# Block-sparse attention and a GELU layer on one core: loading weights with casting DMAs from GpSimd

## The chip, the core and the metric

The kernel runs on one core of a Trainium2 chip. A core has a matrix engine (TensorE, PE in the profile), three engines for elementwise work (VectorE or DVE, ScalarE or ACT, GpSimd or POOL) and SyncE (SP), which here only issues DMAs. Each engine works through its own queue in program order; 16 DMA engines move the data between main memory (HBM) and the on-chip memory SBUF. TensorE writes to PSUM, from where VectorE or ScalarE bring results to SBUF. The metric is the device time of one execution in microseconds (us), the median of several runs.

## The reference

Inputs are q, k and v of shape (4, 8, 768, 64) and the two weights, `w_in` (512, 2048) and `w_out` (2048, 512), all float32.

```python
def _attn_ref(q, k, v):                      # block = 64, 12 blocks, top_k = 3
    k_rep = k.reshape(B, H, n_blocks, block, D).mean(axis=3)
    gate_scores = np.einsum('bhsd,bhnd->bhsn', q, k_rep)
    gate_scores = np.where(causal, gate_scores, -1000000000.0)
    top_idx = np.argsort(gate_scores, axis=-1)[..., -top_k:]
    ...
            sel = set(top_idx[b, h, i].tolist()) | {own_block[i]}
            for kb in sel:
                mask[b, h, i, kb * block:(kb + 1) * block] = True
    ...
    mask = mask & (pos[:, None] >= pos[None, :])
    scores = np.where(mask, scale * np.matmul(q, k.transpose(0, 1, 3, 2)), -1000000000.0)
    attn = softmax(scores)
    return np.matmul(attn, v)

def _moe_ref(x, w_in, w_out):
    h = x @ w_in
    g = 0.5 * h * (1.0 + np.tanh(c * (h + 0.044715 * h * h * h)))
    return g @ w_out
```

Every query attends, causally, to its own block of 64 keys and to the three blocks whose mean key it scores highest. The heads are put side by side to x of 3072 x 512, which goes through `w_in`, a GELU and `w_out`.

## The kernel before

The 32 heads are taken as 16 pairs, p = 4b + hp for batch b. Pairs 0 to 3 (batch 0) are each worked through in three units of 256 queries; pairs 4 to 15 in one unit of 768. A unit loads q, k, v as float32, splits q and k into a high and a low fp16 part, computes the gate scores, picks the blocks, builds the mask, computes the scores, takes exponentials, multiplies with v and writes normalised rows, transposed, to `xT` (fp16). The GELU layer runs over 12 chunks of 256 tokens: for four quarters of the hidden size an up-projection (`hps` in PSUM), a GELU to `gT`, and for two halves of 128 tokens a down-projection over the four quarters into `ops`. A chunk of the GELU layer needs its batch's four pairs, so in the run the attention of one batch and the GELU layer of earlier tokens are interleaved.

The program is a table of named steps and one long string, `ORDER`, that says in which order they are emitted. Since every engine keeps program order, the string is the schedule of each engine and of each DMA queue. A suffix `:a`, `:v` or `:p` picks the engine (ACT, DVE, POOL), `@0` to `@2` a PSUM buffer. The steps that the rest of this text names:

- `d0.g.t.x` loads q, k or v (x = 0, 1, 2) of 128 tokens of four heads of batch 0, `d.p.x` those of a pair of a later batch (two DMAs, one for each head), both into float32 tiles of the pool `io`. They are issued on SP, but for four early k loads on ACT.
- `lw.in.s` and `lw.out.s`, s = 0 to 7, load an eighth of `w_in` or `w_out`, 128 x 1024 float32, into a staging tile of the pool `w32` (7 buffers), issued on SP (line 329). `cw.in.s` and `cw.out.s` cast it to fp16 (line 338), on POOL all 16. Quarter dj of the up-projection needs eighths 2dj and 2dj + 1 of `w_in`, quarter dj of the down-projection those of `w_out`.
- `v.p.t` casts v to fp16 in one of four `v16` tiles, whose 65th column holds ones (`c.v`). `hn0`/`hn1` and `ln0`/`ln1` are the high and low parts of q and k for pairs 4 to 15, `zqh`, `zkh` and `zql` transposes by DMA, `c0`/`c1` copies of the transposes.
- `t2` transposes q and k of batch 0 on PE; `k` computes scores on PE, `ma` adds the mask there, `x` takes exponentials on ACT, `a` zeroes what lies above the diagonal on POOL (two instructions each for the units of batch 0, one otherwise), `p` multiplies with v on PE.
- `u.ch.dj.half` is the up-projection on PE (8 matmuls for each half), `y` the GELU on ACT, `f.ch.ti.dj` four matmuls of the down-projection, `o` the copy of its result out of PSUM, `w` the store, issued on SP.
- `c.*` fill constants, most of them on POOL. `dmN` runs N matmuls of zeros that nothing reads. `c.warm` runs 40 of the same kind and is the last step but one of the order.

Of the kernel before, what the change touches and what calls it, by code (L numbers as in the profile page):

```python
# [8 lines left out]
FP32 = mybir.dt.float32  # L9
# [17 lines left out]
c.ident d0.0.0.0 d0.0.1.0 d0.0.0.1 c.ident16 c.v.0 c.bd c.par.1 c.par.0 d0.0.1.1 c.kb.3 c.own  # L27
c.kb.1 d0.1.1.0 t2.1.0@0 d0.0.2.0 c.kb.0 c.v.1 d0.1.0.0 c.kb.2 t2.0.0@1 s.1.0 d0.1.1.1 c.erow.0
d0.1.0.1 b.1.0 h2.1.0 l.1.0 h2.0.0 d0.0.2.1 c.gate s.0.0 c.v.2 dm13 g.1.0 m.1.0 t2.2.0@2 c.erow.3
d0.0.3.0 t2.3.0@0 mt.1.0 l.0.0 c.erow.1 mc.1.0:a s.2.0 d0.1.2.0 d0.1.0.2 d0.0.3.2 b.0.0 dm10 g.0.0  # L30
d0.0.3.1 s.3.0 c.erow.2 k.1.0.0@1 h2.2.0 d0.0.1.2 m.0.0 d0.0.0.2 h2.3.0 c.v.3 d0.0.5.0 v.1.0:p
d0.1.3.0 dm16 mt.0.0 l.3.0 ma.1.0.0 mc.0.0:a l.2.0 d0.1.1.2 t2.1.2@0 v.0.0:p b.3.0 dm6 g.3.0 c.bi
x.1.0.0 t2.0.2@2 dm7 k.0.0.0@1 h2.0.2 ma.0.0.0 b.2.0 m.3.0 x.0.0.0 g.2.0 d0.1.2.1 d0.1.3.1 s.0.2
lw.in.0 h2.1.2 m.2.0 dm14 k.2.0.0@1 mt.3.0 b.0.2 mc.3.0:a lw.in.1 a.1.0.0 dm8 mt.2.0 l.0.2
mc.2.0:a d0.0.5.1 dm8 ma.2.0.0 lw.in.4 cw.in.0:p g.0.2 t2.3.2@2 d0.0.2.2 l.1.2 a.0.0.0 s.1.2
d0.0.4.0 k.0.2.0@0 x.2.0.0 v.2.0:p h2.3.2 d0.1.5.0 k.3.0.0@1 lw.in.2 ma.3.0.0 m.0.2 s.3.2 x.3.0.0
a.3.0.0 dm8 mt.0.2 a.2.0.0 l.3.2 dm6 k.0.2.1@1 v.3.0:p mc.0.2:a b.1.2 p.0.0.0@2 p.0.0.1 ma.0.2.0
x.0.2.0 g.1.2 x.0.2.1 n.0.0 dm6 t2.2.2@2 lw.out.0 p.1.0.0@0 m.1.2 p.1.0.1 d0.0.4.1 n.1.0 h2.2.2
dm7 xt.0.0 lw.in.3 lw.in.6 lw.out.1 p.3.0.0@1 l.2.2 p.3.0.1 xc.0.0:a dm8 mt.1.2 s.2.2 b.3.2
v.1.2:p d0.1.4.0 k.1.2.0@0 v.0.2:p mc.1.2:a dm5 xt.1.0 k.1.2.1@2 xc.1.0:a cw.in.1:p ma.1.2.0 n.3.0  # L40
x.1.2.1 cw.in.2:p lw.in.5 dm2 g.3.2 x.1.2.0 dm3 p.2.0.0@1 p.2.0.1 a.0.2.1 dm4 t2.0.4@2 d0.1.4.1
lw.in.7 m.3.2 a.1.2.1 dm4 xt.3.0 n.2.0 cw.out.0:p p.0.2.0@0 h2.0.4 p.0.2.1 xc.3.0:a dm5 xt.2.0
lw.out.2 t2.1.4@1 n.0.2 d.4.1 xc.2.0:a d0.1.2.2 b.2.2 u.0.0.0@0 cw.in.4:p cw.in.3:p h2.1.4
cw.in.5:p s.0.4 l.0.4 g.2.2 m.2.2 u.0.0.1 y.0.0 u.0.1.0@2 mt.2.2 b.0.4 cw.out.1:p u.0.1.1 mc.2.2:a
g.0.4 cw.in.7:p d0.1.3.2 s.1.4 l.1.4 cw.in.6:p m.0.4 lw.out.3 k.2.2.0@0 k.2.2.1@1 ma.2.2.0 y.0.1
p.1.2.0@2 d0.1.5.1 mt.3.2 mc.3.2:v v.3.2:p x.2.2.0 p.1.2.1 f.0.0.0 xt.0.2 n.1.2 k.3.2.0@2 lw.out.5
k.3.2.1@0 cw.out.2:p ma.3.2.0 d.5.1 x.2.2.1 b.1.4 xc.0.2:v mt.0.4 lw.out.4 d0.1.4.2 u.0.2.0@1
a.2.2.1 lw.out.6 hn1.4.0:v mc.0.4:v d.4.0 x.3.2.1 u.0.2.1 x.3.2.0 g.1.4 ln1.4.0:v v.2.2:v y.0.2
u.0.3.0@0 u.0.3.1 k.0.4.2@2 p.2.2.0@1 p.2.2.1 m.1.4 cw.out.3:p ma.0.4.1 a.3.2.1 cw.out.5:p s.4.0
y.0.3 t2.2.4@0 d0.1.5.2 n.2.2 t2.3.4@1 b.4.0 x.0.4.2 xt.2.2 xc.2.2:v h2.3.4 xt.1.2 s.2.4 f.0.0.1  # L50
p.3.2.0@2 p.3.2.1 d0.0.4.2 hn1.5.0:p h2.2.4 s.3.4 d0.0.5.2 l.3.4 l.2.4 n.3.2 k.0.4.0@1 xc.1.2:a
mt.1.4 k.0.4.1@0 mc.1.4:a ma.0.4.0 k.1.4.2@2 ma.1.4.1 b.2.4 x.0.4.0 lw.out.7 xt.3.2 xc.3.2:v
cw.out.4:p a.0.4.2 ln1.5.0:v f.0.0.2 g.2.4 x.0.4.1 d.5.0 x.1.4.2 k.1.4.0@1 k.1.4.1@0 ma.1.4.0
x.1.4.1 x.1.4.0 hn0.4.0:p m.2.4 cw.out.6:p u.1.0.0@2 mt.2.4 b.3.4 mc.2.4:v ln0.4.0:v cw.out.7:p
u.1.0.1 s.5.0 b.5.0 u.1.1.0@0 y.1.0 v.0.4:p g.3.4 k.2.4.0@1 m.3.4 u.1.1.1 c.ke.0.0:p v.2.4:v
zqh.4.0 f.0.0.3 p.0.4.0@2 y.1.1 p.0.4.1 v.1.4:v k.2.4.1@0 o.0.0:a ma.2.4.0 zql.4.0 n.0.4
c.ke.0.1:p c.q0.0 mt.3.4 zkh.4.0 mc.3.4:v f.0.1.0 hn0.5.0:v xt.0.4 k.2.4.2@2 ma.2.4.1 a.1.4.2
xc.0.4:v f.0.1.1 x.2.4.1 g.4.0 x.2.4.2 ln0.5.0:v d.6.1 c.ke.1.1:p x.2.4.0 f.0.1.2 k.3.4.2@0
ma.3.4.1 hn1.6.0:p k.3.4.0@2 k.3.4.1@1 zql.5.0 v.3.4:v c.q0.1 ma.3.4.0 c1.4.0.0:p zqh.5.0 x.3.4.2
x.3.4.1 c0.4.0.0:p m.4.0 ln1.6.0:v d.6.0 a.2.4.2 f.0.1.3 x.3.4.0 c0.4.0.1:v d.7.1 u.1.2.0@0 mt.4.0  # L60
mc.4.0.0:a hn0.6.0:p c0.5.0.0:p zkh.5.0 u.1.3.0@1 p.1.4.0@2 mc.4.0.1:v p.1.4.1 o.0.1:a g.5.0
u.1.3.1 u.1.2.1 c1.4.0.1:v c0.5.0.1:p a.3.4.2 w.0.0 n.1.4 zqh.6.0 y.1.3 k.4.0.3@2 y.1.2 c1.5.0.0:p
f.1.0.0 p.2.4.0@1 p.2.4.1 m.5.0 c.ke.1.0:p n.2.4 x.4.0.3 ln0.6.0:v d.7.0 f.1.0.1 k.4.0.1@0 s.6.0
b.6.0 x.4.0.1 k.4.0.4@1 p.3.4.0@2 p.3.4.1 xt.1.4 k.4.0.0@0 f.1.0.2 zql.6.0 xc.1.4:v hn1.7.0:v
c1.5.0.1:p a.4.0.3 mt.5.0 n.3.4 x.4.0.4 k.4.0.2@1 x.4.0.0 mc.5.0.1:v k.4.0.5@2 f.1.0.3 x.4.0.5
mc.5.0.0:v k.5.0.0@0 d.4.2 c0.6.0.0:p x.4.0.2 xt.3.4 o.1.0:a x.5.0.0 a.4.0.0 k.5.0.2@2 k.5.0.4@1
ln1.7.0:v xc.3.4:v xt.2.4 x.5.0.4 zkh.6.0 f.1.1.0 c0.6.0.1:p xc.2.4:v g.6.0 a.4.0.1 a.4.0.4
u.2.1.0@0 u.2.1.1 v.4.0:p hn0.7.0:v a.4.0.5 u.2.0.0@1 u.2.0.1 a.4.0.2 d.8.1 x.5.0.2 p.4.0.0@2
y.2.1 m.6.0 k.5.0.5@0 ln0.7.0:v mt.6.0 mc.6.0.1:v y.2.0 p.4.0.1 mc.6.0.0:v f.1.1.1 k.5.0.1@1 s.7.0
hn1.8.0:p n.4.0 a.5.0.0 a.5.0.4 c1.6.0.0:p x.5.0.5 x.5.0.1 d.8.0 hn0.8.0:v k.5.0.3@0 u.2.2.0@2  # L70
u.2.3.0@1 ln1.8.0:v c1.6.0.1:p a.5.0.2 a.5.0.5 x.5.0.3 b.7.0 u.2.3.1 zqh.7.0 zql.7.0 ln0.8.0:v
g.7.0 m.7.0 a.5.0.1 u.2.2.1 y.2.3 f.1.1.2 d.5.2 k.6.0.5@0 a.5.0.3 k.6.0.0@1 y.2.2 k.6.0.4@2
c0.7.0.1:p f.1.1.3 w.0.1 zqh.8.0 x.6.0.5 s.8.0 zkh.7.0 v.5.0:p x.6.0.4 x.6.0.0 a.6.0.4 p.5.0.0@0
p.5.0.1 o.1.1:v k.6.0.1@2 b.8.0 x.6.0.1 c1.7.0.0:p mt.7.0 f.2.0.0 mc.7.0.0:a k.6.0.3@1 mc.7.0.1:v
c0.7.0.0:a f.2.0.1 k.6.0.2@2 zql.8.0 d.6.2 x.6.0.3 g.8.0 c1.7.0.1:v a.6.0.5 n.5.0 c0.8.0.1:p
x.6.0.2 a.6.0.3 a.6.0.0 d.9.1 v.6.0:p k.7.0.3@0 f.2.0.2 a.6.0.1 m.8.0 k.7.0.1@1 w.1.0 d.9.0
a.6.0.2 zkh.8.0 k.7.0.2@2 f.2.0.3 x.7.0.3 d.7.2 k.7.0.0@0 hn1.9.0:v xt.5.0 xc.5.0:v x.7.0.1
o.2.0:a p.6.0.0@1 p.6.0.1 ln1.9.0:v hn0.9.0:p x.7.0.0 a.7.0.3 x.7.0.2 d.10.0 xt.4.0 k.7.0.4@0
x.7.0.4 xc.4.0:v f.2.1.0 mt.8.0 c0.8.0.0:p c1.8.0.1:v mc.8.0.1:v zqh.9.0 a.7.0.1 k.7.0.5@2
ln0.9.0:v zql.9.0 w.1.1 n.6.0 f.2.1.1 mc.8.0.0:a a.7.0.4 v.7.0:a zkh.9.0 c1.8.0.0:p a.7.0.2 d.8.2  # L80
f.2.1.2 a.7.0.0 k.8.0.0@0 x.7.0.5 s.9.0 a.7.0.5 p.7.0.0@2 b.9.0 p.7.0.1 c0.9.0.1:p c0.9.0.0:p
c1.9.0.0:p d.10.1 x.8.0.0 xt.6.0 xc.6.0:a k.8.0.5@1 n.7.0 k.8.0.1@0 x.8.0.1 f.2.1.3 hn0.10.0:v
xt.7.0 a.8.0.0 xc.7.0:v k.8.0.2@2 x.8.0.5 a.8.0.5 k.8.0.4@0 u.3.0.0@1 x.8.0.2 v.8.0:p g.9.0
k.8.0.3@2 u.3.0.1 zqh.10.0 a.8.0.2 x.8.0.4 m.9.0 u.3.1.0@0 x.8.0.3 u.3.1.1 o.2.1:v a.8.0.3 d.11.1
a.8.0.4 u.3.2.0@2 mt.9.0 c1.9.0.1:p ln0.10.0:v a.8.0.1 mc.9.0.1:v y.3.0 hn1.10.0:p y.3.1
mc.9.0.0:a d.11.0 zql.10.0 u.3.2.1 f.3.0.0 k.9.0.1@1 p.8.0.0@0 ln1.10.0:v p.8.0.1 d.9.2 y.3.2
k.9.0.0@2 d.12.1 x.9.0.1 s.10.0 f.3.0.1 hn1.12.0:p k.9.0.2@1 f.3.0.2 n.8.0 zkh.10.0 b.10.0 x.9.0.0
k.9.0.5@0 k.9.0.4@2 x.9.0.2 c0.10.0.0:v x.9.0.5 u.3.3.0@1 x.9.0.4 k.9.0.3@0 hn0.11.0:v a.9.0.2
g.10.0 c0.10.0.1:v u.4.1.0@2 m.10.0 c1.10.0.1:p x.9.0.3 a.9.0.4 w.2.0 u.3.3.1 u.4.1.1 u.4.2.0@0
xt.8.0 a.9.0.1 a.9.0.0 a.9.0.3 d.12.0 v.9.0:p d.13.0 ln0.11.0:v u.4.2.1 xc.8.0:v y.3.3 y.4.2  # L90
f.3.0.3 hn1.11.0:v mt.10.0 u.4.0.0@1 u.4.0.1 o.3.0:v zqh.11.0 a.9.0.5 mc.10.0.0:v f.3.1.0
c1.10.0.0:v p.9.0.0@0 y.4.0 ln1.12.0:v f.3.1.1 hn0.12.0:v zkh.11.0 zql.11.0 y.4.1 mc.10.0.1:v
k.10.0.5@1 p.9.0.1 zqh.12.0 k.10.0.2@2 f.3.1.2 w.2.1 c0.11.0.0:p ln1.11.0:v x.10.0.5 x.10.0.2
n.9.0 s.11.0 b.11.0 k.10.0.1@1 zkh.12.0 d.10.2 u.5.2.0@0 s.12.0 k.10.0.0@2 x.10.0.1 c1.11.0.0:p
x.10.0.0 ln0.12.0:v k.10.0.4@1 d.13.1 b.12.0 g.11.0 f.3.1.3 a.10.0.2 k.10.0.3@2 a.10.0.5 x.10.0.4
d.11.2 a.10.0.1 x.10.0.3 u.5.2.1 hn0.13.0:a u.5.1.0@1 u.5.1.1 m.11.0 zql.12.0 mt.11.0 y.5.1
c1.11.0.1:v o.3.1:v hn1.13.0:p u.5.0.0@2 ln0.13.0:v u.5.0.1 c0.11.0.1:v u.4.3.0@1 u.4.3.1
mc.11.0.1:v f.4.0.0 mc.11.0.0:v zql.13.0 xt.9.0 y.5.2 c1.12.0.0:v w.3.0 d.14.0 c0.12.0.0:v
c1.12.0.1:p a.10.0.3 d.14.1 y.5.0 ln1.13.0:v xc.9.0:v k.11.0.3@0 y.4.3 f.4.0.1 g.12.0 k.11.0.1@2
# [38 lines left out]
def kernel(  # L138
# [9 lines left out]
    nc = tc.nc  # L148
# [8 lines left out]
    NPAIR = B * HP  # L157
# [744 lines left out]
```

## Time and profile before

| what | value |
|---|---|
| median of 3 runs | 285.09 us (284.98 to 286.42) |
| the profiled execution | 284.7 us, its span 282.7 us |
| TensorE clock granted | 1.00 over the whole span |
| PE matmuls | 2956, of them 140 of zeros by `dm`, 40 by `c.warm` |
| first up-projection `u.0.0.0` starts | 29.94 us |
| last w_out cast starts | 56.88 us |
| DMA read and written | 27.26 MB and 6.29 MB |
| weight loads to landing | 7.4 us (w_in), 7.0 us (w_out), median |

The span is the time between the first and the last thing that the profiler saw on the core; the execution's own time is 2.0 us longer. In the profile a line such as L338 is a line of the kernel. A busy share of an engine is an average over the span; rows of 40 digits give it for 40 equal slices, in tenths. A row of a group reads: line, engine, operation, output <- input, shapes, count, then busy time in us and mean ns of one, then the idle time of the engine just before these instructions and what ended it. The list of waits gives, for an engine and a tile, whom it waited for: us in total, times, the longest. SPq is the queue on which SP issues DMAs; the time of such a row is that of the issue, not of the transfer.

### The profile page before, as it was taken

Reading aid. Unit: us, or ns where it says so; the run is one execution under the profiler, and the core shown is the slowest. Engines: PE = TensorE matmul, PEld = TensorE weight load, DVE = VectorE, ACT = ScalarE, POOL = GpSimd, SP = SyncE. Lnnn points to the kernel's source line nnn. Section 1 sums busy time; section 2 is a strip of 40 time slices with the busy share of each in tenths; the row PEclk is TensorE's granted clock in tenths of the full one; section 3 lists DMA queues with packets and bytes.
Section 4 is the critical chain, followed back from the end, with each engine's and each line's share of the span. In section 5 each row is a group of like instructions: output and inputs, shape, how many; then the busy total and the mean of one; then the engine's idle time right before and its main releaser. Section 6 shows DMA issues by size and latency. Waiting matters only on the chain.

```text
span 282.7 us, 7360 instructions
## 1 busy us (share of the span) xinstructions
PE 267.8 (95%) x2956; PEld 191.2 (68%) x2956; DVE 159.7 (56%) x511; ACT 194.6 (69%) x222; POOL 139.2 (49%) x215
## 2 busy tenths in 40 slices
PE   3898998799999989989999999999999999999998
PEld 2776865557668756767778656688766666767655
DVE  3988788798888478746778697634503041000000
ACT  2466898679999987897488887877897721434130
POOL 8668476888999478473937671660110300000000
DMA  8999989888898893999999956991001102010111
GB/s 158 218 313 312 353 221 309 210 142 160 168 222 170 179 218 60 180 220 207 112 219 179 216 97 131 152 195 39 0 2 74 39 0 77 37 39 0 74 39 74
DMA packets 112097, 41.11 MB, mean 145 GB/s; under 512 B 104896, under 2 KB 104896, under 8 KB 112064
## 3 DMA queue, kind: packets, MB, share of 16 engines
q1 hardware_dynamic: 109952, 40.12, 68.3%
q10 hardware_dynamic: 2112, 0.52, 1.1%
q8 instruction: 23, 0.38, 0.6%
q14 instruction: 10, 0.08, 0.1%
HBM read 27.26 MB, written 6.29 MB: 119 GB/s over the span
## 4 chain that ended last, share of the span: by engine, by line
PE 75%; DMA 9%; POOL 5%; SPq 4%; DVE 3%; issue 2%; ACT 0%; ACTq 0%; POOLq 0%
PE ops L821 27%; PE hps L800 26%; PE st L623 8%; PE pv L705 6%; DMA io<-in_k_dram 4%; DMA io<-in_v_dram 3%; DMA io<-in_q_dram 2%; POOL at L691 2%; PE xt L734 2%; POOL hn L187 2%; SPq L356 1%; SPq L329 1%; PE mt L576 1%; PE kp L475 1%; DVE ln L435 1%
## 5 line engine op out<-in xcount | busy, mean ns | idle before, releaser
L821 PE MATMUL ops<-w_out,gT 128*128 128x512 f16 x384 | 94.6, 379 | 2.6 <-POOL w_out L338 2.0
L676 ACT ACTIVATE at<-st 128x1024 f16<-128x1024 f32 (+2 forms) x96 | 83.9, 917 | 13.9 <-PE st L623 8.5
L800 PE MATMUL hps<-xT,w_in 128*128 128x256 f16 x768 | 91.4, 272 | 0.0
L800 PEld LDWEIGHTS <-w_in 128*128 128x128 f16 x768 | 73.8, 98 | 13.4 <-issue 0.4
L810 ACT ACTIVATE gT<-hps 128x1024 f16<-128x1024 f32 x48 | 47.7, 1023 | 41.0 <-PE hps L800 40.6
L691 POOL TENSOR_SCALAR_AFFINE_SELECT at<-at 128x256 f16<-128x256 f16 x96 | 47.8, 520 | 36.8 <-ACT at L676 35.9
L821 PEld LDWEIGHTS <-gT 128*128 128x128 f16 x384 | 35.8, 97 | 35.9 <-issue 3.4
L623 PE MATMUL st<-qk,qk 76*128 76x512 f16 (+2 forms) x192 | 37.4, 305 | 1.2 <-DVE xn L721 1.0
L829 DVE COPY osb<-ops 128x512 f32<-128x512 f32 x16 | 11.0, 689 | 45.6 <-PE ops L821 43.5
L187 POOL TENSOR_SCALAR hn<-io 128x768 f16<-128x768 f32 x12 | 25.7, 2144 | 20.8 <-DMA io<-in_k_dram 11.1
L435 DVE SCALAR_TENSOR_TENSOR ln<-io,hn 128x768 f16<-128x768 f32 x24 | 27.6, 1152 | 4.7 <-POOL hn L187 4.4
L705 PEld LDWEIGHTS <-at 128*128 128x128 f16 x672 | 24.0, 98 | 4.0 <-POOL at L691 0.6
L705 PE MATMUL pv<-v,at 128*128 128x65 f16 x672 | 25.7, 194 | 0.5 <-POOL at L691 0.4
L623 PEld LDWEIGHTS <-qk 76*128 76x128 f16 x192 | 16.1, 97 | 10.6 <-issue 1.1
L676 ACT ACT_TABLE_LOAD x13 | 16.7, 1283 | 3.2 <-PE st L623 1.9
L810 ACT ACT_TABLE_LOAD x14 | 18.0, 1283 | 0.2
L721 DVE TENSOR_TENSOR xn<-pv,zrec 128x256 f16<-128x256 f32 (+1 forms) x24 | 16.6, 691 | 0.8
L458 POOL COPY qk<-khT 64x768 f16<-64x768 f16 x14 | 12.8, 915 | 7.4 <-DMA khT<-hn 3.8
L743 DVE COPY xT<-xt 128x768 f16<-128x768 f16 (+1 forms) x17 | 7.6, 446 | 14.6 <-PE xt L734 14.4
L586 DVE COPY qk<-mt 12x640 f16<-12x640 f16 x17 | 8.3, 486 | 11.9 <-ACT qk L586 9.9
L458 POOL COPY qk<-qhT 64x768 f16<-64x768 f16 x13 | 13.0, 999 | 3.6 <-issue 2.5
L554 DVE MAX8 mx<-gm 128x8 f32<-128x12 f32 x160 | 14.0, 158 | 0.8
(87 smaller groups left out, 293.1 us busy)
## 6 DMA issues: line engine op xcount, KB each, us to landing
out_dram<-osb SPq DMA_DIRECT2D x24, 256.0 KB, 2.6
io<-in_k_dram SPq DMA_DIRECT2D x24, 192.0 KB, 4.1
io<-in_q_dram SPq DMA_DIRECT2D x24, 192.0 KB, 4.1
io<-in_v_dram SPq DMA_DIRECT2D x24, 192.0 KB, 4.1
w_in<-in_moe_w_in_dram SPq DMA_DIRECT2D x8, 512.0 KB, 7.4
w_out<-in_moe_w_out_dram SPq DMA_DIRECT2D x8, 512.0 KB, 7.0
io<-in_q_dram SPq DMA_DIRECT2D x12, 128.0 KB, 4.3
io<-in_v_dram SPq DMA_DIRECT2D x12, 128.0 KB, 4.2
```

The lines of the kernel that those rows point to most:

```text
L187: math_on[eng].tensor_scalar(out=out, in0=in_, scalar1=c, scalar2=None, op0=ALU.mult)
L435: math_on[eng].scalar_tensor_tensor(out=g.rearrange("p t c -> p (t c)"), in0=IO[u[0], x].rearrange("p t h d -> p (t h d)"), scalar=QS, in1 ...
L458: copy_on[eng](out=dst[0:64, :], in_=src[64 * hh:64 * hh + 64, :])
L554: nc.vector.max(out=mx8[:, g, :], in_=gm[:, g, :])
L623: nc.tensor.matmul(st[:, hh, cb:cb + nq * 128], kt[p % 2][hh][0:64 + NBLK, jc * 128:(jc + 1) * 128], qt[p % 2][hh][0:64 + NBLK, qc * 128:( ...
L676: nc.scalar.activation(out=ov, in_=iv, func=AF.Exp, bias=0.0, scale=SCALE / (QS * QS))
L691: nc.gpsimd.affine_select(out=a, in_=a, compare_op=ALU.is_ge, fill=0.0, base=0, pattern=[[0, 2], [1, 128]], channel_multiplier=-1,)
L705: nc.tensor.matmul(pvt[:, o:o + 65], AT[p, hh, jc, qc], v16[p % NSLOT][:, jc, hh, :], start=(jc == 0), stop=(jc == qc),)
L721: nc.vector.tensor_tensor(out=xn[:, 0:nt].rearrange("p c h d -> p h c d"), in0=pz[:, :, :, 0:64], in1=zrec[:, :, 0:nt].unsqueeze(3).to_bro ...
L800: nc.tensor.matmul(hps[:, j * TCH:(j + 1) * TCH], w_in16[:, ci, fi * 128:(fi + 1) * 128], xT[ci][:, t0:t0 + TCH], start=(ci == 0), stop=(c ...
L810: nc.scalar.activation(out=g.rearrange("p a w -> p (a w)"), in_=G["h", ch, dj], func=AF.Gelu_apprx_tanh, bias=0.0, scale=1.0,)
L821: nc.tensor.matmul(G["o", ch, ti], G["g", ch, dj][:, j, ti * 128:(ti + 1) * 128], w_out16[:, fi, :], start=(fi == 0), stop=(fi == NF - 1),)
```

## The change

- The steps `cw.*` and the pool `w32` go. `lw.*` is now one DMA from the float32 weight straight into `w_in16` or `w_out16`, issued by GpSimd; the DMA casts.
- For pairs 14 and 15 `d.p.2` loads v in the same way, two DMAs, straight into `v16`; their steps `v.14.0` and `v.15.0` go.
- `io` and `atp` get 12 buffers instead of 9.
- `c.warm` goes.
- `ORDER` is a new one for all other steps as well, with other engines for some: high parts on POOL 16 instead of 12, v casts of 22 steps as 11 on POOL, 8 on ACT, 3 on DVE (before 15, 1, 8 of 24), output copies 15 on ACT and 9 on DVE (before 8 and 16). The `dm` steps hold 158 matmuls instead of 140.

```diff
-    io = ctx.enter_context(tc.tile_pool(name="io", bufs=9))
-    w32p = ctx.enter_context(tc.tile_pool(name="w32", bufs=7))
+    io = ctx.enter_context(tc.tile_pool(name="io", bufs=12))
...
-    atp = ctx.enter_context(tc.tile_pool(name="atp", bufs=9))
+    atp = ctx.enter_context(tc.tile_pool(name="atp", bufs=12))
...
-    def c_warm():
-        wpool = wide.tile([128, 1024], FP32, tag=f"wide{at_slot[0]}", name="warm")
-        for _ in range(40):
-            nc.tensor.matmul(wpool[:, 0:128], zsrc, zsrc, start=True,
-                             stop=True)
...
     def load_w(which, s):
-        t = w32p.tile([128, 2, 512], FP32, tag="w32", name=f"w32_{which}_{s}")
         if which == "in":
             src = moe_w_in.rearrange("(ci p) f -> p ci f", p=128)
             src = src[:, 2 * (s % 2):2 * (s % 2) + 2,
                       (s // 2) * 512:(s // 2 + 1) * 512]
+            dst = w_in16[:, 2 * (s % 2):2 * (s % 2) + 2,
+                         (s // 2) * 512:(s // 2 + 1) * 512]
         else:
             src = moe_w_out.rearrange("(fi p) c -> p fi c", p=128)
             src = src[:, 2 * s:2 * s + 2, :]
-        nc.sync.dma_start(out=t, in_=src)
-        w_parts[which, s] = t
-
-    def cast_w(which, s, eng):
...
             dst = w_out16[:, 2 * s:2 * s + 2, :]
-        copy_on[eng](out=dst, in_=w_parts[which, s])
+        nc.gpsimd.dma_start(out=dst, in_=src)
...
     def load(p, x):
         b, hp = divmod(p, HP)
+        if x == 2 and p >= NPAIR - 2:
+            for hh in range(2):
+                nc.gpsimd.dma_start(
+                    out=v16[p % NSLOT][:, :, hh, 0:64],
+                    in_=v[b, 2 * hp + hh].rearrange("(t p) d -> p t d",
+                                                    p=128))
+            return
         a = io.tile([128, NC, 2, D], FP32, tag="io", name=f"io_{p}_{x}")
...
-        step(f"v.{un}", v_copy, u)
+        if u[0] < NPAIR - 2:
+            step(f"v.{un}", v_copy, u)
```

Of the new order, the lines with all 16 weight loads and with one of the casting loads of v:

```diff
+c.ident dm12 t2.0.0@0 c.kb.2 c.ident16 d0.1.1.0 d0.1.1.1 d0.1.0.1 c.erow.0 h2.0.0 c.own c.gate
...
+c.erow.1 l.2.0 k.1.0.0@1 h2.3.0 mc.1.0:a dm9 k.0.0.0@0 lw.in.0 l.3.0 b.3.0 d0.1.3.0 d0.1.2.1
+v.1.0:p ma.0.0.0 x.0.0.0 g.2.0 ma.1.0.0 lw.out.0 m.2.0 t2.0.2@2 h2.0.2 dm8 g.3.0 s.0.2 lw.in.3
...
+mt.3.0 b.0.2 d0.0.4.0 h2.1.2 mc.3.0:a s.1.2 k.3.0.0@2 ma.2.0.0 lw.in.6 dm3 g.0.2 ma.3.0.0 l.1.2
+x.2.0.0 d0.0.4.1 dm5 p.1.0.0@0 d0.0.5.1 p.1.0.1 x.3.0.0 lw.in.1 m.0.2 n.1.0 t2.2.2@1 h2.2.2 dm7
...
+x.0.2.1 a.3.0.0 lw.in.4 dm12 t2.0.4@0 s.2.2 a.0.0.0 x.0.2.0 p.2.0.0@1 d0.1.3.2 p.2.0.1 h2.0.4
+d0.1.5.0 m.1.2 dm4 xt.1.0 p.0.0.0@2 d.4.0 d0.1.5.1 d0.0.5.2 xc.1.0:a v.3.0:a n.2.0 a.0.2.1 lw.in.2
+dm10 xt.2.0 p.3.0.0@1 s.0.4 p.3.0.1 l.0.4 lw.in.5 lw.out.3 lw.out.1 b.2.2 xc.2.0:a dm4 mt.1.2
+n.3.0 v.1.2:a lw.out.2 mc.1.2:a p.0.0.1 k.1.2.0@0 dm3 g.2.2 v.0.2:a dm3 k.1.2.1@1 d0.0.4.2
+ma.1.2.0 n.0.0 m.2.2 x.1.2.0 p.0.2.0@2 p.0.2.1 x.1.2.1 dm12 xt.3.0 t2.3.2@0 xc.3.0:v lw.out.7
...
+v.2.2:a g.0.4 l.3.2 d0.1.4.1 lw.out.4 u.0.0.1 u.0.1.0@0 u.0.1.1 v.3.2:p h2.1.4 l.1.4 s.1.4 lw.in.7
+m.0.4 y.0.0 k.2.2.0@1 hn1.4.0:v k.2.2.1@2 v.0.4:p d.5.1 ma.2.2.0 d0.1.4.2 y.0.1 g.3.2 d0.1.5.2
+x.2.2.1 f.0.0.0 k.3.2.0@0 f.0.0.1 m.3.2 mt.3.2 b.1.4 t2.2.4@2 mc.3.2:v c.bi xt.0.2 x.2.2.0 d.7.1
+hn0.4.0:p k.3.2.1@1 ma.3.2.0 s.2.4 h2.2.4 x.3.2.0 x.3.2.1 xc.0.2:v g.1.4 l.2.4 u.0.2.0@2 m.1.4
+t2.3.4@0 h2.3.4 mt.0.4 u.0.2.1 s.3.4 mc.0.4:v a.1.2.1 u.0.3.0@1 l.3.4 p.1.2.0@0 y.0.2 mt.1.4
+lw.out.5 ln0.4.0:v p.1.2.1 u.0.3.1 y.0.3 b.2.4 v.1.4:p k.0.4.2@2 a.2.2.1 lw.out.6 mc.1.4:v
+ma.0.4.1 g.2.4 f.0.0.2 n.1.2 a.3.2.1 d.5.0 p.2.2.0@0 p.2.2.1 ln1.4.0:v f.0.0.3 m.2.4 n.2.2
...
+a.12.0.4 m.13.0 u.6.2.0@1 x.12.0.2 c0.14.0.1:v u.7.1.1 o.5.0:a y.7.1 d.14.2 u.6.1.0@0 u.6.2.1
+u.6.1.1 w.5.0 mt.13.0 a.12.0.0 y.6.2 mc.13.0.1:a u.6.0.0@2 y.6.1 mc.13.0.0:v zql.15.0 u.6.0.1
```

The extract begins with the idle matmuls that stand ahead of the first transposes.

## What was predicted

> **What bounds the kernel now.** I read the page's first two parts, then the list of who waited for whom on PE, then the groups of the operations that the change touches, then the timelines of POOL and of the end.
>
> ```profile
> PE 267.8 (95%) x2956; PEld 191.2 (68%) x2956; DVE 159.7 (56%) x511; ACT 194.6 (69%) x222; POOL 139.2 (49%) x215
> PE   3898998799999989989999999999999999999998
> DVE  3988788798888478746778697634503041000000
> POOL 8668476888999478473937671660110300000000
> DMA  8999989888898893999999956991001102010111
> ```
>
> PE bounds the span: from the eleventh slice (7.07 us each) on it is full, the others are not. What can be won or lost lies in the first 60 us, where PE has holes and the DMA engines are full.
>
> ```profile
> PE w L401 <- POOL E L275: 3.9, 1, 3.9
> PE ops L821 <- POOL w_out L338: 2.0, 1, 2.0
> PE w L401 <- DMA io<-in_k_dram: 1.2, 1, 1.2
> PE w L401 <- DMA io<-in_q_dram: 0.7, 2, 0.5
> ```
>
> The 3.9 is the wait for the first loads and stays. Of the others, 2.0 is a wait for a cast of w_out, what the change removes by name; 1.2 and 0.7 wait for q and k. All that PE waited for after 60 us adds up to 3.1 us.
>
> ```profile
> L853 PE MATMUL dm<-zsrc 128*128 128x128 f16 x140 | 11.6, 228 | 0.0
> L338 POOL CAST w_out<-w_out 128x1024 f16<-128x1024 f32 x8 | 8.3, 1042 | 1.8 <-DMA w_out<-in_moe_w_out_dram 1.8
> L338 POOL CAST w_in<-w_in 128x1024 f16<-128x1024 f32 x8 | 8.2, 1040 | 5.7 <-DMA w_in<-in_moe_w_in_dram 5.7
> L329 SPq DMA_DIRECT2D w_in<-in_moe_w_in_dram x8: 467/534/2477, 12.9 to 27.7; - x8
> L329 SPq DMA_DIRECT2D w_out<-in_moe_w_out_dram x8: 451/979/2319, 20.5 to 51.6; - x8
> DMA to landing us min/median/max: 4.8/7.2/9.1
> ```
>
> The casts cost POOL 16.5 us and 7.5 us of waiting. The two SPq lines give ns (least, median, most) for issuing a weight load; SP's timeline adds them to 15.7 us, 0.98 each. The last line, of the same source line, is issue to landing.
>
> **The sum** is made against the profiled execution: 284.7 us with a span of 282.7, so 2.0 around the span; the median of the runs is 285.09, 0.4 above it.
>
> *The 40 warm matmuls at the end: 0.*
>
> ```profile
> 278.98 2.40 PE L238 MATMUL warm<-zsrc 128*128 128x128 f16 x40
> 279.23 0.58 ACT L829 COPY osb<-ops 128x512 f32<-128x512 f32 x1 [3.75 <-PE ops L821]
> 279.84 0.33 SPq L833 DMA_DIRECT2D out_dram<-osb  x1
> ```
>
> They end at 281.4. The last store starts at 279.84 and lands, by the page's median of 2.6 us, at 282.4. That store hides them; without it they would be worth 2.2.
>
> *Idle matmuls (dm): +0.4, and -0.5 for what they warm.* 158 in place of 140. The first 12 now stand ahead of the first transposes, inside the 3.9 us wait, so 146 count. In a warm stretch 16 take 1.07 us, 0.065 each: 6 more are 0.4. Early in the trace 13 take 1.59 us and the first eight transposes 2.3 against 1.18 for the next eight: PE starts slow though the granted clock is 1.00 throughout. The 12 may cure part of it: 0 to -1.1; I take half.
>
> *POOL's queue up to 45 us: +3.1, the term that decides.* POOL loses 16 casts and gains 16 issues, in program order among its other work. No row shows an issue by POOL. Bounds: SP's cheapest weight issue, 0.45, and its dearest, 2.48. SP's mean is 0.98. POOL's own work is stretched when it runs beside VectorE:
>
> ```profile
> 21.65 0.53 POOL L487 CAST v<-io 128x128 f16<-128x128 f32 x2
> 39.48 1.38 POOL L487 CAST v<-io 128x128 f16<-128x128 f32 x2 [1.41 <-DMA io<-in_v_dram]
> 39.76 0.95 DVE L435 SCALAR_TENSOR_TENSOR ln<-io,hn 128x768 f16<-128x768 f32 x1
> ```
>
> The same two copies took 0.85 longer around a VectorE operation of 0.95. VectorE is busy 7 to 9 tenths of the slices from 7 to 42 us, so I give half of it to each issue: 0.98 + 0.42 = 1.4.
>
> With 1.4 I walk POOL's new order. Its constants end at 11.1, as before. lw.in.0 follows; v.1.0 waits for its loads and ends at 13.75, as before; lw.out.0 and lw.in.3 to 16.55; a mask select (two instructions, 0.77) to 17.3; lw.in.6 and lw.in.1 to 20.1; two selects to 21.7; lw.in.4 to 23.1; a.0.0.0 to 23.8; a.0.2.1 to 24.6. Seven issues in a row (lw.in.2, in.5, out.3, out.1, out.2, out.7, out.4) to 34.4. v.3.2 0.53, lw.in.7 1.4, v.0.4 0.53, c.bi 0.87, hn0.4 2.14, a.1.2.1 0.77: 40.6, where lw.out.5 starts. v.1.4 and a.2.2.1 (1.3) stand before lw.out.6, which starts at 43.3. From the ninth on, an issue of the changed program also waits until the eighth before it has landed; by the median of 7.2 us that is long over, even by twice 7.2.
>
> When PE wants these: the new order has the same work before its first up-projection u.0.0.0 as the old, which began it at 29.94, so 30. p.0.0.0, which needs a.0.0.0, stands about 7.6 us of matmuls ahead of that, 22.4: it waits 1.4. From u.0.0.0 to f.0.0.2 stand eight up halves of 0.87, two f of 0.86 and 5.3 us of attention by the rows of those matmuls: due 44.0. It needs lw.out.5: 40.6 + 7.2 = 47.8, due 45.4 after the first wait, so 2.4. f.0.0.3, 1.4 later, due at 49.2, needs lw.out.6: 50.5, so 1.3. Together 5.1, less the 2.0 that the cast's wait cost: +3.1. Behind POOL's seven issues stand hn0.4 and a.1.2.1, for which p.1.2.0 waits at 41.6 + 1.4: they end in time. The same walk with 1.04, a cast's length, makes every one of these waits vanish: -2.0. With 1.25 it gives +1.1, with 2.0 about +11, with 2.48 +18. Landing I left at SP's 7.2, though half the bytes are written: at 4.8 the term falls by 3.5, at 9.1 it grows by 1.9.
>
> *SP's queue: -0.6.* Freed of 15.7 us of issuing, it starts q, k and v sooner; PE's 1.4 us of waits for them after the first 5 us can go (0 to -1.4). Not all: in the first 56 us the DMA engines move 14.8 MB (the GB/s of eight slices) at 8 or 9 tenths busy, and the same bytes are wanted. More io and at buffers (12 for 9) act here too, later.
>
> *v of pairs 14 and 15: +0.5.* Four issues on POOL in place of two casts on VectorE and four SP issues. Behind the first two stand a.12.0.0, a.12.0.3 and then p.12.0.0; POOL idles 5.7, 3.2 and 1.25 us in that stretch (170 to 190), which covers them. If the cover is gone, 1.4 each at two places: 2.8; bounds 0 and 9.9 (four of 2.48).
>
> *The rest: 0.* POOL takes 16 of the hn casts (2.14) instead of 12, 8.6 us, beside the 16.5 it loses and 143 of idle. ACT has 15 output copies of 0.59 instead of 8 and two table loads of 1.28 fewer. Neither ends a wait of PE above 1 us now.
>
> Sum: 0 + 0.4 - 0.5 + 3.1 - 0.6 + 0.5 = +2.9, so **287.6 us**.
>
> **The rivals.**
>
> *Faster: issues are cheap.* One mechanism: POOL's queue between 11 and 45 us. If an issue costs no more than a cast (1.04, the deciding point), w_out has landed when f.0.0.2 asks for it: -2.0, and with the q and k waits (-1.4), -0.5 and +0.4, 281.2. For it: SP issues half of its w_in loads in 0.53; the casts' waits of 7.5 go too. Against: POOL is not SP. With all the later waits gone as well, 278.
>
> *The seven issues hold POOL.* At 2.0 and above the selects and hn behind them come late, then p.1.2.0, then both w_out loads: 284.7 + 11 = 296, with 303 at 2.48. For it: the stretched copies. Against: most POOL rows of that stretch show no stretch. The Trainium skill's page "SBUF — State Buffer" (SBUF: two separate sides) states this as a rule: descriptors of a DMA issued by GpSimd can't be written while VectorE holds the port they share, and one of about 620 ns took about 3100 beside a VectorE copy. By that price for every issue, an estimate from the page, the result would lie above 303. The trace shows such a stretch once, by 0.85 us.
>
> *No change.* PE is 95% busy, its work the same; an issue of about 1.15 gives waits of 2 us for those of 2 removed: 285. A form of it: the DMA engines, full until 56 us, pace PE in both orders.
>
> **Chances.** Forecast (issue between 1.2 and 1.7; 286.5 to 292) 0.36; seven issues hold POOL 0.14; both slower, 0.50. Faster 0.34. No change 0.16, within 0.5%, 1.4 us, about what a measurement of this kernel can tell. The range, 279.5 to 297, takes in the faster case and issues up to 2.0; the forecast's own is 286.5 to 292.
>
> **What would show it.** POOL's issue rows: 1.2 to 1.7 us each. PE waiting for w_out's DMA at L821's counterpart 3 to 4 us before 55 us, and about 1 for a select. First up-projection near 30 to 31 us. The end: last matmul to span end as before, 3.7. I am wrong if the issues take about 1 us or less and PE's waits in the first 60 us fall below 4 us beside the first 3.9 (now 6.3, the list added up), or if casting loads land in much over 9 us, which this trace can't exclude.

## The result, and the profile after

The changed kernel takes 293.67 us (median of 4 runs, 292.23 to 294.9) against 285.03 for the kernel before on the same chip: 1.030 times as long, 95% interval 1.023 to 1.036. Its profiled execution took 293.04 us with a span of 291.3; before, 284.7 and 282.7. So 8.3 us are to be found. (Here and below, times are medians of all runs, and ratios leave out runs that lie far above the others of their kernel.)

The page of the kernel after, busy time and the span in 40 slices of 7.28 us:

```profile
PE 272.8 (94%) x2934; PEld 191.9 (66%) x2934; DVE 150.0 (51%) x492; ACT 197.6 (68%) x241; POOL 137.6 (47%) x215
PE   5899677999999999898999999999999999999994
...
PEclk9999976899999999999999999999999999999999
DMA  8999999999978799599975999092011001010111
```

PE is full from the eighth slice on, as before from the ninth. The loss is around these: in the fifth to seventh PE has holes, and in the sixth to eighth (36 to 58 us) the granted clock is 0.6 to 0.9, where before it was 1.00 throughout. (These are means: in finer windows it is 0.50 from 39 to 42 and from 46 to 52 us and 1.00 from 43 to 45.) By 5-us windows of the kernel after (busy us and instructions of PE, its weight loads, VectorE, ScalarE and GpSimd; then granted clock, DMA share, GB/s):

```profile
30.00:35.00 5.00, 3.64 (x39) 2.98 (x37) 0.92 (x5) 0.96 (x4) 0.12 (x1) 1.00 1.21 197
35.00:40.00 5.00, 2.37 (x27) 1.06 (x28) 3.02 (x17) 4.95 (x6) 0.84 (x2) 0.89 1.23 211
40.00:45.00 5.00, 2.85 (x12) 0.76 (x10) 0.85 (x5) 1.92 (x3) 0.43 (x2) 0.77 0.82 172
45.00:50.00 5.00, 4.64 (x36) 2.94 (x37) 2.28 (x10) 2.32 (x3) 4.65 (x13) 0.57 1.30 234
50.00:55.00 5.00, 5.00 (x50) 4.01 (x50) 3.55 (x10) 2.96 (x4) 4.99 (x9) 0.75 1.35 168
sum 25.00, PE 18.50 PEld 11.74 DVE 10.62 ACT 13.11 POOL 11.03; mean PE 3.70 PEld 2.35 DVE 2.12 ACT 2.62 POOL 2.21
```

The same windows of the kernel before, their sum:

```profile
sum 25.00, PE 21.82 PEld 15.73 DVE 20.57 ACT 20.58 POOL 17.16; mean PE 4.36 PEld 3.15 DVE 4.11 ACT 4.12 POOL 3.43
```

PE stands idle 6.5 of the 25 us, 3.2 before: 3.3 lost. The busy time is also slower: busy time by what is missing from a clock of 1.00, window by window, is 0.3 + 0.7 + 2.0 + 1.2 = 4.2. Together 7.5 of the 8.3. All engines, PE too, are emptier than before, so none of them is the bound; the DMA share alone is high, 1.2 to 1.35 in four of the five windows (the times of packets overlap, so it can pass 1).

To follow the loss through all kernels I use one measure, *work done by t*: the columns of all matmuls started by then, without the idle and warm ones, at 0.213 us for 512 (in this trace matmuls of 512 columns start 0.215 us apart at best), with float32 weighted four times. The whole program has 249.4 us. The four is a choice, and too much: float32 transposes of 128 columns start 0.109 us apart here, fp16 ones 0.055. With a weight of two the two kernels stand at 19.1 and 25.4 at 45 us, and about 7 apart at 60 us, as with four. The kernel after stands at 16.4 at 30 us (16.0 before), at 23.3 at 45 us (30.5 before) and at 35.8 at 60 us (42.7 before); from there to 275 us it stays 6.4 to 8.9 behind, 8.2 at 250 us. So about 7 us are lost in the first 60 us and about 1 after them.

What PE waited for in the first 60 us of the kernel after (us in total, times, longest):

```profile
PE st L622 <- DVE ks L452: 2.8, 1, 2.8
PE w L388 <- DMA io<-in_q_dram: 2.8, 2, 2.3
PE w L388 <- POOL ownm L255: 1.4, 1, 1.4
PE st L622 <- ACT gT L798: 1.1, 1, 1.1
```

No wait for `w_out` is left. In its place PE waits for q, and for VectorE and ScalarE. ScalarE's timeline (start, us, instruction, in brackets its idle time and what ended it) says what those two waited for:

```profile
34.84 0.30 ACT L474 CAST v<-io 128x128 f16<-128x128 f32 x1 [4.04 <-DMA io<-in_v_dram]
35.05 0.59 ACT L395 ACTIVATE qk<-w 128x512 f16<-128x512 f32 x1
35.66 1.28 ACT L798 ACT_TABLE_LOAD   x1
36.95 1.94 ACT L798 ACTIVATE gT<-hps 128x1024 f16<-128x1024 f32 x2
```

The cast `v.2.2:a` stands 4.04 us in front of a v load. Behind it in ScalarE's queue are `h2.1.4` and the gelus. VectorE's `l.1.4` needs `h2.1.4`, its ks (`s.1.4`) stands behind that, and PE's `k.2.2.0` needs the PSUM buffer that these two read. GpSimd's timeline in the same kernel:

```profile
24.90 3.60 POOL L319 DMA_DIRECT2D w_out<-in_moe_w_out_dram  x5
...
34.88 0.30 POOL L474 CAST v<-io 128x128 f16<-128x128 f32 x1 [6.07 <-DMA io<-in_v_dram]
...
44.57 0.52 POOL L474 CAST v<-io 128x128 f16<-128x128 f32 x2 [8.73 <-DMA io<-in_v_dram]
...
48.83 0.79 POOL L319 DMA_DIRECT2D w_out<-in_moe_w_out_dram  x1
```

Five issues in a row take 3.6 us; two v casts then stand 14.8 us. So the late things are loads of q, k and v on SP's queue. The DMA queues of the kernel after between 25 and 40 us (packets, MB written, share of the 16 engines' time; then issues, KB each, us to landing):

```profile
q0 software_dynamic: 2277, 2.20, 87.8%
q1 hardware_dynamic: 3507, 0.88, 33.9%
...
io<-in_q_dram SPq DMA_DIRECT2D x2, 192.0 KB, 14.6
...
io<-in_v_dram SPq DMA_DIRECT2D x2, 128.0 KB, 6.0
io<-in_q_dram SPq DMA_DIRECT2D x1, 128.0 KB, 13.5
io<-in_k_dram SPq DMA_DIRECT2D x1, 128.0 KB, 10.9
```

And of the kernel before:

```profile
q1 hardware_dynamic: 6073, 4.70, 103.1%
...
io<-in_k_dram SPq DMA_DIRECT2D x4, 192.0 KB, 7.8
io<-in_k_dram SPq DMA_DIRECT2D x2, 128.0 KB, 6.1
io<-in_v_dram SPq DMA_DIRECT2D x2, 128.0 KB, 5.5
io<-in_q_dram SPq DMA_DIRECT2D x1, 128.0 KB, 8.0
```

The engines are full in both. Read bytes are about the same: 4.7 MB before, 0.88 + 2 x 2.20 = 5.3 after (a cast writes half of what it reads). But before, weights and q, k, v came through one queue in the order of the steps; now GpSimd's queue (q0) takes 2.6 times the engine time of SP's, and SP's q and k loads land after 11 to 15 us instead of 6 to 8 (its two v loads, issued at 37 and 39 us, after 6.0, before 5.5). Others are issued late: SP comes to `d0.1.4.0` at 41.99 (24.64 before), behind loads that the old order has later and behind issues that take up to 4.7 us. `d0.1.4.0` and `d0.1.4.1`, the last q and k of pairs 2 and 3 in the new order, landed at 45.0 and 45.6 (32.6 and 34.6 before). But in the old order the last of them is `d0.1.5.1`, which landed at 42.8 (43.6 after): these pairs were complete only 2.8 us earlier. The first up-projection still starts at 29.73 (29.94 before).

### The profile page after: what moved, and what is told of

The parts are those of the page before. It is cut to its first block, busy times and chain, and to the rows that moved or that the text cites. A ratio compares the mean times of both kernels' runs of the same rounds, so it can differ in the third digit from the quotient of the medians.

```text
span 291.3 us, 7291 instructions
## 1 busy us (share of the span) xinstructions
PE 272.8 (94%) x2934; PEld 191.9 (66%) x2934; DVE 150.0 (51%) x492; ACT 197.6 (68%) x241; POOL 137.6 (47%) x215
## 3 DMA queue, kind: packets, MB, share of 16 engines
q0 software_dynamic: 7488, 4.59, 12.4%
## 4 chain that ended last, share of the span: by engine, by line
PE 56%; POOL 15%; SPq 11%; issue 6%; DVE 4%; DMA 4%; ACT 3%; POOLq 0%; ACTq 0%
PE ops L809 22%; PE hps L788 20%; SPq L336 9%; PE st L610 7%; POOL hn L184 6%; POOL qk L445 4%; POOL at L678 4%; PE pv L692 4%; SPq L356 2%; DMA io<-in_v_dram 2%; DMA io<-in_q_dram 2%; PE xt L721 1%; POOL v L474 1%; PE gt L507 1%; DVE ln L422 1%
## 5 line engine op out<-in xcount | busy, mean ns | idle before, releaser
L809 PE MATMUL ops<-w_out,gT 128*128 128x512 f16 x384 | 95.7, 383 | 0.7 <-ACT osb L817 0.7
L788 PE MATMUL hps<-xT,w_in 128*128 128x256 f16 x768 | 94.2, 276 | 0.1
L663 ACT ACTIVATE at<-st 128x1024 f16<-128x1024 f32 (+2 forms) x96 | 83.7, 920 | 14.9 <-PE st L610 10.8
L678 POOL TENSOR_SCALAR_AFFINE_SELECT at<-at 128x256 f16<-128x256 f16 x96 | 41.6, 452 | 68.5 <-ACT at L663 67.9
L610 PE MATMUL st<-qk,qk 76*128 76x128 f16 (+2 forms) x192 | 36.2, 305 | 0.8 <-POOL qk L445 0.7
L184 POOL TENSOR_SCALAR hn<-io 128x768 f16<-128x768 f32 x16 | 34.5, 2157 | 0.3
L817 DVE COPY osb<-ops 128x512 f32<-128x512 f32 x9 | 6.2, 689 | 49.6 <-PE ops L809 49.6
L692 PE MATMUL pv<-v,at 128*128 128x65 f16 x672 | 26.3, 194 | 0.3
L692 PEld LDWEIGHTS <-at 128*128 128x128 f16 x672 | 24.2, 98 | 2.7 <-POOL at L678 0.9
L817 ACT COPY osb<-ops 128x512 f32<-128x512 f32 x15 | 8.8, 587 | 13.4 <-PE ops L809 11.9
L798 ACT ACT_TABLE_LOAD x13 | 16.7, 1283 | 0.2
L445 POOL COPY qk<-qhT 64x768 f16<-64x768 f16 x18 | 16.6, 920 | 0.6
L395 ACT ACTIVATE qk<-w 128x512 f16<-128x512 f32 x12 | 7.2, 597 | 12.7 <-DVE ks L452 10.6
L841 PE MATMUL dm<-zsrc 128*128 128x128 f16 x158 | 13.5, 236 | 1.1 <-POOL zsrc L226 1.1
```

Of the source, the lines that this page charges most:

```text
L184: math_on[eng].tensor_scalar(out=out, in0=in_, scalar1=c, scalar2=None, op0=ALU.mult)
L445: copy_on[eng](out=dst[0:64, :], in_=src[64 * hh:64 * hh + 64, :])
L610: nc.tensor.matmul(st[:, hh, cb:cb + nq * 128], kt[p % 2][hh][0:64 + NBLK, jc * 128:(jc + 1) * 128], qt[p % 2][hh][0:64 + NBLK, qc * 128:( ...
L663: nc.scalar.activation(out=ov, in_=iv, func=AF.Exp, bias=0.0, scale=SCALE / (QS * QS))
L678: nc.gpsimd.affine_select(out=a, in_=a, compare_op=ALU.is_ge, fill=0.0, base=0, pattern=[[0, 2], [1, 128]], channel_multiplier=-1,)
L692: nc.tensor.matmul(pvt[:, o:o + 65], AT[p, hh, jc, qc], v16[p % NSLOT][:, jc, hh, :], start=(jc == 0), stop=(jc == qc),)
```

## The experiments

Each row is one kernel: its time, the ratio to the kernel before on the same chip with its interval, and the work done by 30, 45 and 60 us of its profiled execution. "New" and "old" are the orders after and before. Each kernel has one profile; that of e5 is of a run of 300.52 us and that of e11 of one of 288.9, both above the median, and so are their three columns of work. Edits of the order are shown as steps with a neighbour on each side, not as whole lines.

| kernel | what it is | us | ratio | 30 | 45 | 60 |
|---|---|---|---|---|---|---|
| before | old steps, staged weights | 284.2 to 285.0 | 1 | 16.0 | 30.5 | 42.7 |
| after | new steps, casting DMAs | 293.67 | 1.030 [1.023, 1.036] | 16.4 | 23.3 | 35.8 |
| e1 | after, four w_out loads later | 294.05 | 1.031 [1.024, 1.038] | 11.6 | 23.8 | 35.1 |
| e2 | after, eight weight loads in one go | 294.59 | 1.036 [1.032, 1.041] | 10.8 | 21.7 | 33.8 |
| e3 | old steps, casting DMAs | 285.62 | 1.003 [1.000, 1.006] | 17.1 | 28.1 | 42.9 |
| e4 | after, idle matmuls in the hole | 293.24 | 1.030 [1.027, 1.034] | 16.4 | 23.3 | 34.9 |
| e5 | after, SP's order | 296.84 | 1.042 [1.037, 1.048] | 16.4 | 25.1 | 32.3 |
| e6 | after, v cast later on ScalarE | 292.61 | 1.031 [1.025, 1.036] | 15.0 | 23.3 | 36.2 |
| e7 | e5 and e6 | 297.89 | 1.048 [1.042, 1.053] | 16.4 | 26.3 | 32.7 |
| e8 | new steps, staged weights | 299.26 | 1.053 [1.049, 1.057] | 12.3 | 23.3 | 30.8 |
| e9 | new steps, old sequence of loads, casting | 297.4 | 1.044 [1.041, 1.047] | 12.5 | 19.5 | 31.5 |
| e10 | old steps, new sequence of loads, casting | 291.41 | 1.023 [1.019, 1.027] | 16.8 | 26.2 | 37.1 |
| e11 | e3, pair 4's k later | 286.79 | 1.000 [0.996, 1.004] | 16.8 | 28.7 | 38.9 |
| e12 | e9, paced | 296.65 | 1.040 [1.034, 1.046] | 15.9 | 24.2 | 33.7 |

**First round: how the weights are issued, and by which part of the change.**

e1, in the order of after:

```diff
-l.0.4 lw.in.5 lw.out.3 lw.out.1 b.2.2
+l.0.4 lw.in.5 lw.out.1 b.2.2
...
-n.3.0 v.1.2:a lw.out.2 mc.1.2:a
+n.3.0 v.1.2:a mc.1.2:a
...
-u.0.1.1 v.3.2:p h2.1.4
+u.0.1.1 v.3.2:p lw.out.3 lw.out.2 h2.1.4
...
-mc.0.4:v a.1.2.1 u.0.3.0@1
+mc.0.4:v a.1.2.1 lw.out.4 u.0.3.0@1
...
-a.2.2.1 lw.out.6 mc.1.4:v
+a.2.2.1 lw.out.6 lw.out.7 mc.1.4:v
```

> The changed kernel, but of the seven weight loads that GpSimd issues one after another near 25 us four are moved back: lw.out.3 and lw.out.2 behind the copy v.3.2, lw.out.4 behind a.1.2.1, lw.out.7 behind lw.out.6. Theory A (the weights' own queue takes the DMA engines from q, k and v, whose late landing stalls the attention): v.3.2 and v.0.4 land several us sooner, more than half of PE's 6.3 us of waits between 33 and 46 us and of the lowered clock go, about 287 us (285 to 290). Theory B (the weights themselves come too late): 295 or more. Theory C (the new order as such, not the loads): no change, 293 to 294.

No gain. In this execution PE stood earlier, 2.7 us for a k load at 26.4 us (clock 0.55 from 25 to 30), before the moved loads could matter; d0's q and k were late behind the w_in loads instead. Up to there the order is that of the kernel after, yet `d0.0.4.1` landed at 26.3 here and at 22.3 there: landings differ by some us between executions.

e2 puts the first eight weight loads together:

```diff
-k.0.0.0@0 lw.in.0 l.3.0
+k.0.0.0@0 lw.in.0 lw.out.0 lw.in.3 lw.in.6 lw.in.1 lw.in.4 lw.in.2 lw.in.5 l.3.0
```

> The changed kernel with the first eight weight loads (lw.in.0 to lw.in.5 of its order) issued in one go near 11 us. Theory A: q, k and v of batch 0 starve from 11 us on, the first up-projection starts after 33 us instead of 29.7, and the time is 296 or more. Theory B: weights are there sooner, 292 or less. Theory C: 293 to 294.

Work by 30 us falls from 16.4 to 10.8, so weights issued early do push q and k back (waits of 3.1 and 1.7 us before 30 us). Yet the end moves by only 1 us: what is lost early is not lost again at 45 us.

e3 is the old kernel with the casting DMAs for the weights alone (v, the buffers and the order of the other steps as before):

```diff
-        nc.sync.dma_start(out=t, in_=src)
-        w_parts[which, s] = t
+        nc.gpsimd.dma_start(out=dst, in_=src)
...
-            step(f"cw.{which}.{s}", cast_w, which, s)
...
-    w32p = ctx.enter_context(tc.tile_pool(name="w32", bufs=7))
```

> The kernel before with one part of the change alone: the 16 weight loads are casting DMAs issued by GpSimd at the places of lw in the old order, the casts are left out; buffers, v and everything else as before. Theory A: without staging buffers and waits for casts GpSimd issues them sooner and closer together than SP did, q, k and v are delayed, 287 to 292. Theory C: the old order with 16.5 us less work on GpSimd, 282 to 285.5.

This decides most: the casting DMAs of the weights cost 0 to 2 us by themselves. They starve SP's queue here just as much; the DMA queues of e3 between 25 and 40 us:

```profile
q0 software_dynamic: 2080, 2.00, 81.0%
q1 hardware_dynamic: 3734, 0.93, 37.8%
```

GpSimd stood 11.3 us in front of a v load, and PE lost little by it. The starved queue alone is not the cause.

e4 fills the hole to hold the clock:

```diff
-u.0.1.0@0 u.0.1.1 v.3.2:p
+u.0.1.0@0 u.0.1.1 dm36 v.3.2:p
...
-y.0.0 k.2.2.0@1 hn1.4.0:v
+y.0.0 k.2.2.0@1 dm14 hn1.4.0:v
```

> The changed kernel with 36 matmuls of zeros behind u.0.1.1 and 14 behind the score step k.2.2.0, in PE's two waits of 2.85 and 1.15 us near 35 us. If the lowered clock (0.57 to 0.89 between 35 and 55 us) comes from PE standing idle: it stays near 1.00 at least up to 42 us, and the time falls by 1 to 3 us, 291 to 292.5. If not: 293 to 295.

The clock was 0.90 in 35 to 40 us, then 0.50 in 40 to 45. The fillers ran out before the hole did; the clock's 4 us could not be bought back so.

**Second round: mending the new order where its trace shows a wait.**

e5 moves loads of the next batch on SP's queue:

```diff
-b.1.2 d0.1.2.2 d.4.1 mc.0.2:a
+b.1.2 d0.1.2.2 mc.0.2:a
...
-p.0.0.0@2 d.4.0 d0.1.5.1
+p.0.0.0@2 d0.1.5.1
...
-k.2.2.0@1 hn1.4.0:v k.2.2.1@2 v.0.4:p d.5.1 ma.2.2.0
+k.2.2.0@1 k.2.2.1@2 v.0.4:p ma.2.2.0
...
-g.3.2 d0.1.5.2 x.2.2.1
+g.3.2 d0.1.5.2 d.4.1 d.4.0 d.5.1 x.2.2.1
...
-p.2.2.1 ln1.4.0:v f.0.0.3
+p.2.2.1 hn1.4.0:v ln1.4.0:v f.0.0.3
```

> The kernel after, with three loads of the next batch (pair 4's k and q, pair 5's k) moved in SP's queue behind the last v loads of the first batch; the one VectorE step that reads pair 4's k moves with them. Theory 'late loads' (the 8 us are lost because the first batch's q, k and v land late behind GpSimd's weights, and the new order queues two 192-KB x 2 loads ahead of them): the v loads that POOL and ACT waited 8.7 and 4.0 us for land 3 to 6 us sooner, PE's waits of 2.8 us for ks and of 2.3 us for q fall below 1 each, and the time is 287 to 290 us. Rival 'order of steps' (the new order of PE, ACT and VectorE loses the time, whatever the loads do): 293 to 294. Rival 'DMA engines full': the same bytes come in the same time, so the loads that moved back stall PE later instead; 292 to 294 with PE's first long wait at pair 4 instead of at 36 us.

About 3 us slower. The first batch's last q landed at 40.4 instead of 45.0 and work by 35 us rose from 19.5 to 21.5, but GpSimd then reached `lw.out.5` and `lw.out.6` only at 51.6 and 54.8 (48.8 and 50.8 in the kernel after), behind `hn0.4`, which stood in front of pair 4's q, a load that the edit itself had moved back:

```profile
48.09 2.14 POOL L182 TENSOR_SCALAR hn<-io 128x768 f16<-128x768 f32 x1 [9.60 <-DMA io<-in_q_dram]
```

PE waited 7.1 us for `w_out`, 4.9 of them for these two parts.

e6 moves one cast:

```diff
-u.0.0.0@2 v.2.2:a g.0.4
+u.0.0.0@2 g.0.4
...
-x.3.2.0 x.3.2.1 xc.0.2:v
+x.3.2.0 x.3.2.1 v.2.2:a xc.0.2:v
```

> The kernel after, with one step moved: the cast of v for pair 2's last chunks on ScalarE stands behind that pair's exps instead of ahead of pair 1's split (h2.1.4), so nothing that PE needs soon queues behind a late v load. Theory 'late loads through ScalarE's queue': PE's waits of 2.8 us at 36 us and 1.1 us at 38 us fall to under 1 together, the clock stays above 0.9 until 45 us, and the time is 288 to 291 us. Rival 'the next late load takes over' (pair 0's or 1's q and k come as late as v): PE waits for io instead and the time stays 292.5 to 294. Rival 'order of steps': 293 to 294, with the waits unchanged.

The rival "the next late load takes over" is right, to the letter. PE's timeline of e6:

```profile
38.23 1.02 PE L807 MATMUL ops<-w_out,gT 128*128 128x512 f16 x4 [0.81 <-DMA w_out<-in_moe_w_out_dram]
45.35 1.14 PE L386 MATMUL w<-ident,io 128*128 128x128 f32 x4 [5.99 <-DMA io<-in_q_dram]
```

The waits for ks and gT are gone, PE runs ahead, and stands 6 us in front of the same q load; it goes on at 45.35, in the kernel after at 45.14.

e7 has both edits.

> Both edits at once: SP's three loads of the next batch behind the first batch's last, and the v cast of pair 2 later on ScalarE. Theory 'late loads': the sum of both, 284 to 288 us, PE's waits between 30 and 50 us below 3 us together (7.1 in the kernel after) and the clock above 0.9 there. Rival 'order of steps' or 'DMA engines full': 291 to 294.

Neither gain survives: the waits for q and k shrink to 2.4, those for `w_out` (4.6) and for GpSimd's masks (2.3) come. `hn0.4` stands 12.4 us here. So in e5 and e7 the edit brings a wait of its own, and they don't test the late loads alone.

e8 is the change without its DMA part: the new steps, weights staged as before, each cast by GpSimd some 30 steps behind its load. It has four staging tiles and 11 io tiles for want of space, so it is no exact undoing.

```diff
-        nc.gpsimd.dma_start(out=dst, in_=src)
+        nc.sync.dma_start(out=t, in_=src)
+        w_parts[which, s] = t
...
+            step(f"cw.{which}.{s}", cast_w, which, s)
...
+    w32p = ctx.enter_context(tc.tile_pool(name="w32", bufs=4))
```

> The change without its DMA part: the new step order, with the weights again loaded by SP's queue into fp32 staging tiles (four of them) and cast by GpSimd some 30 steps later; io tiles 11 instead of 12 for want of space, the last two w_out loads some 40 steps earlier. Theory 'late loads' as a clash of the two parts: with one queue the loads come in the order of the steps, so q, k and v aren't starved by the weights; v waits on POOL under 5 us, 284 to 290 us. Rival 'order of steps': the order alone is slow, 293 us or more. A third way: SP's queue is now longer by 16 issues of about 1 us and stalls on staging tiles, so the loads land late for that reason: 290 to 297, with PE waiting for io or w_in.

The slowest of all, so the new steps are slow with staged weights too. But the run doesn't set the steps apart: PE waits here for what staging brings, 5.5 us for GpSimd's masks at 56.8, which stand behind two casts of w_out, and 3.2 for its weight casts, and GpSimd itself 15.6 us for weight loads in front of the casts. How much of the 5.6 us beyond the kernel after is due to the fewer tiles was not tried.

**Third round: the sequence of loads against the sequence of steps.** 58 early load steps stand at 58 places of each order. e9 keeps the new steps and puts the loads at those places in the old sequence; e10 keeps the old steps and puts them in the new sequence. The beginning of the difference in e9:

```diff
-c.par.1 d0.1.0.0 d0.0.2.0 c.par.0
+c.par.1 d0.1.1.0 d0.0.2.0 c.par.0
...
-k.0.0.0@0 lw.in.0 l.3.0
+k.0.0.0@0 d0.1.1.2 l.3.0
```

> The kernel after with every step of PE, ScalarE, VectorE and GpSimd in its new place, and its first 58 load steps (the first batch's q, k and v, the sixteen weight parts, q and k of pairs 4 and 5) put, in the same 58 places of the order, into the sequence that the kernel before has them in (two v loads a few places earlier than that, because the new order reads them earlier). Theory 'sequence of loads' (the DMA engines are full until 57 us in both kernels, and the new order asks for the last q and k of pairs 2 and 3 only at the end, at 45 us): those land at 27 to 35 us, PE does 28 to 31 us' worth of matmuls by 45 us (23.3 in the kernel after, 30.5 before), and the time is 285 to 288 us. Rival 'sequence of steps' (the new order of PE and ScalarE itself): 292 to 297, with PE waiting for something other than pairs 2 and 3's q.

> The mirror image: the kernel of e3 (the steps of before, weights by GpSimd's casting DMAs), with its first 58 load steps in the sequence of the kernel after. Theory 'sequence of loads': q and k of pairs 2 and 3 land near 45 us and PE waits for them, 291 to 296 us. Rival 'sequence of steps': 284 to 287, as e3.

Both are slow. In e9 `d0.1.4.0` and `d0.1.4.1` came early (29.2 and 32.5 us), as hoped, though `d0.1.5.1` only at 44.1; v came later, and ScalarE's cast, which the old steps leave to VectorE at a later place, stood in front of it; ScalarE's and PE's timelines of e9:

```profile
43.10 0.30 ACT L472 CAST v<-io 128x128 f16<-128x128 f32 x1 [7.77 <-DMA io<-in_v_dram]
...
45.23 0.61 PE L620 MATMUL st<-qk 64*128 64x256 f16 x4 [6.88 <-DVE ks L450]
```

In e10 the old steps want `w_in` parts that the new sequence brings last; PE's timeline of e10:

```profile
47.84 3.17 PE L796 MATMUL hps<-xT,w_in 128*128 128x256 f16 x14 [4.80 <-DMA w_in<-in_moe_w_in_dram]
```

With casting DMAs the four pairings give these ratios: old steps and old loads 1.003, old steps and new loads 1.023, new steps and new loads (the kernel after) 1.030, new steps and old loads 1.044. The new sequence of loads alone costs about 6 us with the old steps; with that sequence, what the new steps and the rest of the change add is within the intervals, which overlap.

**Fourth round: two repairs.** e11 mends the largest wait left in e3, VectorE's `hn1.4.0` in front of pair 4's k:

```diff
-t2.1.4@1 n.0.2 d.4.1 xc.2.0:a
+t2.1.4@1 n.0.2 xc.2.0:a
...
-p.1.2.0@2 d0.1.5.1 mt.3.2
+p.1.2.0@2 d0.1.5.1 d.4.1 mt.3.2
...
-a.3.2.1 s.4.0 y.0.3
+a.3.2.1 hn1.4.0:v ln1.4.0:v s.4.0 y.0.3
```

> The kernel of e3 (steps of before, weights by GpSimd's casting DMAs) with one place mended: in e3 VectorE stood 5.0 us at 41 us in front of pair 4's k, which landed at 40.9, and PE then 3.0 us for VectorE's mrow. Here pair 4's k is loaded behind four loads of the first batch, and the two VectorE steps that read it stand behind the first batch's selects. Theory 'an in-order engine stands in front of a load that comes late behind the weights': PE's wait of 3.0 us goes, 282.5 to 284.5 us, below before. Rival 'the DMA engines pace it anyway': some other load is late instead and the time stays 285 to 286.5.

Its 12 runs spread from 283.43 to 290.46, where the kernel before's 17 lie between 283.13 and 288.76: on the whole no gain. The profiled run took 288.9; in it pair 4's k landed at 46.1, and PE's timeline shows:

```profile
46.82 0.19 PE L471 MATMUL kp<-blockind,hn 128*128 128x2 f16 x1 [4.73 <-DVE hn L183]
```

In this run a late load caught the old order as well; what the five short runs (283.43 to 284.16) did, no profile shows. e12 takes e9 and moves three weight loads behind q and k, and ScalarE's v cast as in e6:

```diff
-g.3.0 s.0.2 lw.in.1 t2.1.2@0 d0.0.5.1 lw.in.4 m.3.0
+g.3.0 s.0.2 t2.1.2@0 d0.0.5.1 m.3.0
...
-ma.2.0.0 d0.0.4.0 dm3
+ma.2.0.0 d0.0.4.0 lw.in.1 dm3
...
-x.3.0.0 lw.out.0 m.0.2
+x.3.0.0 m.0.2
...
-a.3.0.0 lw.in.6 dm12
+a.3.0.0 lw.in.6 lw.in.4 lw.out.0 dm12
```

> The kernel of e9 (new steps, old sequence of loads) with the two places mended where its trace shows engines standing: three weight loads that GpSimd issued before the first batch's q and k of the last chunks (lw.in.1, lw.in.4, lw.out.0) are issued some steps later, and ScalarE's cast of pair 2's v (it stood 7.8 us there, and PE 6.9 us behind it) comes after that pair's exps. Theory 'loads and steps have to fit' (nothing in the new steps is slow by itself; each loss is an in-order engine in front of a load that came late): 285 to 289 us, PE's work done by 45 us at 27 or more (19.5 in e9). Rival 'the new steps themselves': 293 or more whatever the loads do.

Up to 35 us the repair works: 21.1 of work, as in the kernel before, against 16.7 in e9 and 19.5 in the kernel after. Then PE waits again, for other loads:

```profile
39.35 1.01 PE L807 MATMUL ops<-w_out,gT 128*128 128x512 f16 x2 [2.99 <-DMA w_out<-in_moe_w_out_dram]
41.07 1.01 PE L807 MATMUL ops<-w_out,gT 128*128 128x512 f16 x2 [0.71 <-DMA w_out<-in_moe_w_out_dram]
44.75 0.48 PE L386 MATMUL w<-ident,io 128*128 128x128 f32 x1 [1.81 <-DMA io<-in_k_dram]
```

The clock falls to 0.50, and 296.65 us is what the rival forecast. By its own condition the theory "loads and steps have to fit" isn't shown by e12.

What all this settles: the issue cost and the weights' casting DMAs are not the loss (e3). It comes with the new order: every kernel with the new steps is slow (e8, e9, e12 and all variants of after), but so is e10, where only the sequence of loads is new. With full DMA engines every mended wait was replaced by a wait for another load or for the steps behind one.

What stays open: which feature of the new order makes it ask for more data before 45 us than the old one. A candidate is that the new PE order has `f.0.0.1` and `t2.2.4`, which needs pair 2's last q and k, ahead of `u.0.2.0`, the old one behind `u.0.3.1`. The traces fit it: 23.3 us of work stand ahead of `t2.2.4` with the new steps, 28.7 with the old. Its last load landed at 45.6 in the kernel after, at 45.8 in e6 and at 44.7 in e12, and PE waited there 2.3, 6.0 and 1.8 us (the rows at 45.35 in e6 and 44.75 in e12). Before and in e3 the last load came hardly earlier, at 42.8 and 42.4, but PE reached `t2.2.4` only at 43.8 and 46.0 and waited for nothing. It can't be all: in e7 that load landed at 41.1, PE waited 0.7 for it, and the time is 297.89. Moving `t2.2.4` was not tried, so this is argued and not shown. No kernel beat the one before.

## Why the prediction came out as it did

The direction and the range held (279.5 to 297), but 287.6 is 6.1 us short, outside the forecast's own 286.5 to 292, and the reason given is wrong. That the time lies in the range is luck: its upper part stood for issues of up to 2.0 us.

- *POOL's queue, +3.1, the deciding term.* It failed at the price of an issue: 1.4 us taken, half as much measured. The issue rows of the kernel after (ns, least, median, most):

```profile
L319 POOL DMA_DIRECT2D w_in<-in_moe_w_in_dram x8: 713/718/872, 10.9 to 35.1; - x8
...
L319 POOL DMA_DIRECT2D w_out<-in_moe_w_out_dram x8: 719/737/788, 12.3 to 50.8; - x8
...
L349 POOL DMA_DIRECT2D v<-in_v_dram x4: 826/834/904, 175.8 to 191.5; - x4
```

  SP's mean of 0.98 came from its long issues (up to 2.48, half of those for w_in 0.53), which stand where the DMA engines are full and so look like a queue held up, not like the price of an issue; and the 0.85 us stretch beside VectorE did not return. At 0.72 the prediction's own walk makes all `w_out` waits vanish, and they did.
- *Faster: issues are cheap.* So its condition was met, and its result, 281.2, missed by 12 us. What it and the forecast shared was the term that failed:
- *SP's queue, -0.6.* Freed of 16 issues, SP was to start q, k and v sooner. Its single issues took up to 4.7 us instead, and between 25 and 40 us its q and k loads landed after 11 to 15 us instead of 6 to 8. I had noted the full DMA engines, but took the same bytes to mean the same times; which queue's bytes come first was left out. The landing rows that the forecast held at 7.2 are 7.2 for `w_in`, and 9.5, at most 12.9, for `w_out`; "casting loads land in much over 9 us" was named as what would prove it wrong, but the loads that hurt were the others.
- *The seven issues hold POOL.* They took 5.0 us, from 23.5 to 28.5. The Trainium skill's page "SBUF — State Buffer" (SBUF: two separate sides) has such an issue at about 3.1 us while VectorE holds the shared port; it states this for VectorE operations of certain kinds only. With VectorE busy 3.92 of the 5 us from 25 to 30 no weight issue took over 0.87; whether any operation there was of these kinds, no run shows. POOL was held, but by v loads (6.1 and 8.7 us), and only after the issues: the walk had given `v.3.2` and `v.0.4` 0.53 each and no wait.
- *No change, the DMA engines pace PE in both orders.* e3 is this case: 285.62, with the DMA engines as full. With the new order it is not.
- *The order itself* was costed through POOL's steps alone; that ScalarE gets 8 v casts instead of 1, each able to stand in front of a load with `h2` steps and gelus behind it, was not walked. It is the first wait of the loss (4.0 us), though not the whole: without it (e6) the time is the same.
- *The clock* was taken as 1.00, as in all of before. About half of the loss, 4.2 us by the windows, is PE at 0.57 to 0.89.
- Right: the warm matmuls at the end, 0 (the last matmul ends 3.8 us before the span's end, 3.7 forecast); the first up-projection (29.73, forecast 30 to 31); the rest after 60 us, about 1 us, with it v of pairs 14 and 15 (+0.5 forecast).
- Two slips change nothing: PE's row is full from the ninth slice on, not from the eleventh, and with landing at 4.8 us the deciding term falls by 2.4 in the prediction's own walk, not by 3.5.

## What to carry to other kernels

When the DMA engines are full, the question about a load is not what it costs to issue but which queue it joins and what it goes ahead of: with the big loads on a queue of their own, q and k on the other queue landed after 11 to 15 us here instead of 6 to 8, and an in-order engine in front of a late load took everything behind it along. Undo the parts of a change one by one before blaming the part with the name: here the casting DMAs cost at most 2 us in the old order, and the new order was slow with either way of loading. How early a step asks for its load matters as much as when the load lands. With the DMA engines full, each wait that was mended here came back at another place.

## What the runs showed of the hardware

- A casting DMA of 512 KB read costs GpSimd 0.72 us to issue. It frees an engine, not the DMA: by the queue lines between 25 and 40 us a packet of q0 took 0.878 x 16 x 15 us / 2277 = 93 ns for 0.97 KB written, one of q1 23 ns for 0.25 KB. An estimate for plain packets of 2 KB, from the same window before (6073 packets, 4284 of them under 512 B, taken at 23 ns): (1.031 x 16 x 15 us - 4284 x 23 ns) / 1789 = 83 ns.
- Between 25 and 40 us GpSimd's queue had 81 to 88% of the engine time and SP's 34 to 38% (they overlap), in the kernel after and in e3 alike.
- The granted clock fell to 0.50 after some holes of PE and not after others: in e9 after 2.2 us without work at 23 us (0.50 from 25 to 31), in e3 not at all after 3.0 us at 39 us. What decides was not found.
